# Second pair's mask rows on ScalarE's DMA queue, its preparation one step nearer, slot zeros from the second pair on

## The chip, the cores and the metric

The kernel runs on one core of a Trainium2 chip. The metric is device time in microseconds (us) of one launch, given as the median of several executions. A profile is one more execution, with its own time.

## The reference

Three layers follow each other: clustered attention, a mixture of experts with a carried choice of expert, and a gated causal convolution. Only the first, on which the change bears, is shown with more than a line.

```python
# q, k, v: 2 x 8 heads x 768 x 64; centroids: 8 heads x 16 x 64
q_assign = argmax(einsum('bhsd,hcd->bhsc', q_n, c_n)); k_assign = likewise for k
mask = q_assign[:, :, :, None] == k_assign[:, :, None, :]
scores = where(mask, 0.125 * q @ k^T, -1e9); attn = softmax(scores)
x = attn @ v                       # heads joined to 512 columns, 1536 tokens
e = argmax(x @ w_gate), or the expert of the token before where a local gate says so
y[token] = softmax(logits)[e] * (relu(x @ w1[e]) @ w2[e])
out = (sigmoid(causal_conv(y)) * (y @ w_val)) @ w_out
```

## The kernel before

**Attention, step by step.** The 16 heads are worked in 8 pairs of two heads. A pair has 12 items (2 halves of the queries, 3 tiles of 128 queries, 2 heads), so there are 96 items and 96 steps of one loop (L750). Step i issues the scores of item i+2 (S, L609 and L613: two matmuls over 128 rows and two over 80 rows, with a row maximum on VectorE, L620), the six transposes of item i on TensorE (T, L644), their two copies out of PSUM (L647 on VectorE or L649 on ScalarE; `act_only` says which), and the exponential of item i+2 on ScalarE (E, L629). From step 7 on, every odd step also issues the products with v of the half before (L656). Every engine executes its own instructions strictly in the order in which this loop writes them; nothing reorders them.

**The operands of the scores.** For each head of a pair there is a tile `st` with four planes of 768 columns: high and low parts of k and q over 128 rows, and in rows 64 to 79 of planes 2 and 3 the *mask rows*, the one-hot clusters of q and k. The last two score matmuls (L613, 80 rows) read them, so a masked score is built by TensorE itself. The first two (L609) do not need them.

**Preparation of the next pair (`prep_steps`).** Its parts, in six groups that the loop hands out one per step: (0) `k_hi` on ScalarE (L333) and `dots1` on TensorE (L351), which reads both halves of `xkq`, the loaded k and q; (1) `q_hi` on ScalarE (L336), `k_lo` on GpSimd (L339), `dots2` on TensorE (L361); (2) the argmax over clusters on VectorE, first part; (3) `q_lo` on VectorE (L342) and `stack1`, six DMAs of 384 KB that copy the parts into both `st` tiles (L406 to L408); (4) argmax, second part; (5) `rows` on TensorE (L390), `rows_out` on ScalarE (L400, writes `ohr`), and `stack2` for both heads, four DMAs of 48 KB that copy the mask rows from `ohr` into `st` (L412, L413). The index of the group is `i % 12 - (0 if g else 2)`: in the first pair, g = 0, the preparation of the second pair runs in steps 2 to 7; in later pairs it runs in steps 0 to 5 of the pair. The first item of the second pair is item 12, whose S is issued in step 10.

**Loads and zeros.** All of the DMAs named so far are issued by SyncE (SP), in program order. `xkq` and `vt` of the second pair are issued ahead of the loop (L82, L83, L88); `xkq` of the third in step 8. `fill_slots` (L148 to L158) writes zeros and a padding number to the two DRAM tables of token slots, 13 DMAs of 514 KB, one at each of the steps 0, 1, 10 and 11 of a pair until they are used up; ahead of the first, GpSimd sets the source tile `padrow`. Tokens are scattered into these tables from step 57 on. Step 7 of the first pair also converts the convolution's weights (`conv_weights`): seven small instructions on VectorE, one on ScalarE (L265), and two on VectorE that wait for it (L266, L267).

Of the kernel before, what the change touches and what calls it, by code (L numbers as in the profile page):

```python
# [8 lines left out]
F32 = mybir.dt.float32  # L9
# [23 lines left out]
def routed_attention_moe_kernel(  # L33
# [12 lines left out]
    nc = tc.nc  # L46
# [277 lines left out]
    def prep_steps(g):  # L324
# [3 lines left out]
        st = [st_p.tile([128, 4, S], F32R, tag=f"st{h}", name=f"st{h}") for h in range(2)]  # L328
# [80 lines left out]

        def stack2(h):  # L410
            r = o["ohr"].bitcast(F32)
            nc.sync.dma_start(st[h][64:80, 2, :].bitcast(F32), r[32 + 16 * h:48 + 16 * h, :])  # L412
            nc.sync.dma_start(st[h][64:80, 3, :].bitcast(F32), r[16 * h:16 * h + 16, :])  # L413

        def S0(h, parts=None):

# [186 lines left out]
    def do_S(i):  # L603
        g, qb, t, h = items[i]
        st = ST[g][h]
        q0 = 384 * qb + 128 * t
        ps = ps_s.tile([128, 2, 512], F32, tag="s", name="s")
        for n in range(2):
            nc.tensor.matmul(  # L609
                ps[:, n, :384], st[:, 1, q0:q0 + 128], st[:, 0, 384 * n:384 * n + 384], start=True, stop=False  # L610
            )
        for n in range(2):
            nc.tensor.matmul(  # L613
                ps[:, n, :384], st[0:80, 2, q0:q0 + 128], st[0:80, 3, 384 * n:384 * n + 384], start=False, stop=True
            )
        row_max(i, ps)
# [6 lines left out]
    def do_exp(i):  # L623
        g, qb, t, h = items[i]
        ps, mx = S_.pop(i)
        if (t, h) == (0, 0):
            Zt[i // 6] = small.tile([128, 3, 2], F32, tag="z", name="z", bufs=4)
        pt = p_p.tile([128, 2, 384], F32, tag="p", name="pexp", bufs=3)
        nc.scalar.activation(  # L629
            pt, ps[:, :, :384], AF.Exp, bias=mx[:, 0:1], accum_out=Zt[i // 6][:, t, h:h + 1]  # L630
        )
        P_[i] = pt.rearrange("p a b -> p (a b)")

    def do_T(i, act_only):
        g, qb, t, h = items[i]
        u = i // 6
        if t == 0:
            PT[u, h] = pt_p.tile([128, NQT, 384], F32, tag=f"pt{h}", name=f"pt{h}")
        p = P_.pop(i)
        for half in range(2):  # L640
            tp = ps_t.tile([128, 3, 128], F32, tag="t", name="tp")
            for k in range(3):
                kt = 3 * half + k
                nc.tensor.transpose(tp[:, k, :], p[:, 128 * kt:128 * kt + 128], ident)  # L644
            dst = PT[u, h][:, 3 * half:3 * half + 3, 128 * t:128 * t + 128]
            if half == 0 and not act_only:
                nc.vector.tensor_copy(dst, tp)  # L647
            else:
                nc.scalar.copy(dst, tp)  # L649

    def do_PV(u, kt):
        g, qb = items[6 * u][:2]
        if kt == 0:
            PVs[u] = ps_v.tile([128, 384], F32, tag="pv", name="pv")
        for h in range(2):
            nc.tensor.matmul(  # L656
                PVs[u][64 * h:64 * h + 64, :], Vt[g][:, kt, h, :], PT[u, h][:, kt, :],
                start=(kt == 0), stop=(kt == NQT - 1), skip_group_check=True,
            )
# [3 lines left out]
    def post1(u):  # L663
        ut = u_p.tile([128, 384], F32, tag="u", name="ut")
        nc.scalar.copy(ut, PVs.pop(u))  # L665
        U_[u] = ut
        for h in range(2):
            PT.pop((u, h))

    def post2(u):  # L670
        g, qb = items[6 * u][:2]
        b, p = pairs[g]
        ut = U_.pop(u)
        z = Zt.pop(u)
        rz = small.tile([128, 3, 2], F32, tag="rz", name="rz")
        nc.vector.tensor_scalar(rz, z, 1e-9, None, op0=ALU.add)
        nc.vector.reciprocal(rz, rz)
        po = ps_m.tile([128, 512], F32, tag="m", name="po")
        pv = po[:, :438].rearrange("p (t c) -> p t c", t=3)
        for t in range(3):  # L680
            nc.tensor.matmul(pv[:, t, :], ut[:, 128 * t:128 * t + 128], wgl_sb[:, p, :], start=True, stop=True)
        t0 = 6 * b + 3 * qb
        nc.vector.tensor_tensor(
            lall[:, t0:t0 + 3, 2 * p:2 * p + 2, :],
            pv[:, :, 128:146].rearrange("p t (h c) -> p t h c", h=2),
            rz.unsqueeze(3).to_broadcast([128, 3, 2, 9]), op=ALU.mult,
        )
        nc.vector.tensor_tensor(
            xnat[:, t0:t0 + 3, 128 * p:128 * p + 128].rearrange("p t (h d) -> p t h d", h=2),
            pv[:, :, 0:128].rearrange("p t (h d) -> p t h d", h=2),  # L690
            rz.unsqueeze(3).to_broadcast([128, 3, 2, 64]), op=ALU.mult,
        )
# [57 lines left out]
    for i in range(NI):  # L750
        g, qb, t, h = items[i]
        u, j = divmod(i, 6)
        if i % 12 == 0:
            prep = prep_steps(g + 1) if g + 1 < 8 else []
        if i + 2 < NI:
            do_S(i + 2)
        do_T(i, act_only=i % 12 in (2, 3, 4, 5, 6, 9) or u >= U - 1)
        if i + 2 < NI:
            do_exp(i + 2)
        if u == U - 1:  # L760
            if j < 2:
                for kt in range(3):
                    do_PV(u - 1, 3 * j + kt)
            if j == 1:
                post1(u - 1)
        elif u and j % 2:
            for kt in (j - 1, j):
                do_PV(u - 1, kt)
            if j == 5:
                post1(u - 1)  # L770
        ps = i % 12 - (0 if g else 2)
        if 0 <= ps < len(prep):
            for f in prep[ps]:
                f()
        if i in (54, 66):
            route = route_steps(i // 12 - 4)
        if j == (0 if u == U - 1 else 4 if i // 12 in (4, 5) else 3) and u > 1:
            post2(u - 2)
        if i == 6 * U - 4:
            post2(u - 1)  # L780
            route = route_steps(2)
        if 6 <= i % 12 <= 9 and i // 12 in (4, 5) or 2 <= j and u == U - 1:
            for _ in range((1, 3, 2, 3)[i % 12 - 6 if i // 12 in (4, 5) else j - 2]):
                route.pop(0)()
        if u == U - 1 and j >= 2:
            if j in (2, 4):
                last_PV(j // 2 - 1)
        if i % 12 == 8 and g + 2 < 8:
            load_kq(g + 2)
        if i % 12 == 7 and 0 < g < 7:  # L790
            load_v(g + 1)
        if i % 12 in (0, 1, 10, 11):
            next(fill, None)
        if i == 7:
            conv_weights()
        if i == 82:
            w_dma(0)
        if i in (84, 88):
            w_split(0, (i - 84) // 4, nc.gpsimd)
        if i == 90:  # L800
            w_dma(1)
# [495 lines left out]
```

## Time and profile before

| | |
|---|---|
| time, median of 3 executions | 572.93 us (572.6 to 576.06) |
| profiled execution: its own time | 573.4 us |
| profiled execution: span of the profile | 571.7 us (1.7 us of the time lie around it) |
| busy: TensorE, ScalarE, VectorE, GpSimd | 546.9, 338.9, 386.9, 115.1 us |
| mean granted clock of TensorE | 0.982 of full speed |
| first pair, steps 0 to 11 | from 18.3 us to about 48 us of the span |

Times inside the profile are us from the start of its span. In a timeline row stand the start, the duration, the engine (PE is TensorE's matmuls, PEld its weight loads, DVE VectorE, ACT ScalarE, POOL GpSimd; SPq and ACTq are the DMA issues of SyncE's and ScalarE's queues), the line, the operation with what it writes and reads, how many instructions are merged into the row, and in brackets the engine's idle time just before and what ended it. A DMA issue's duration is the time that its queue's sequencer was taken up, not the transfer's.

### The profile page before, as it was taken

Reading aid. Unit: us, or ns where it says so; the run is one execution under the profiler, and the core shown is the slowest. Engines: PE = TensorE matmul, PEld = TensorE weight load, DVE = VectorE, ACT = ScalarE, POOL = GpSimd, SP = SyncE. Lnnn points to the kernel's source line nnn. Section 1 sums busy time; section 2 is a strip of 40 time slices with the busy share of each in tenths; the row PEclk is TensorE's granted clock in tenths of the full one; section 3 lists DMA queues with packets and bytes.
Section 4 is the critical chain, followed back from the end, with each engine's and each line's share of the span. In section 5 each row is a group of like instructions: output and inputs, shape, how many; then the busy total and the mean of one; then the engine's idle time right before and its main releaser. Section 6 shows DMA issues by size and latency. Waiting matters only on the chain. (4 is left out here: it accounts for less than half of the span.)

```text
span 571.7 us, 9383 instructions
## 1 busy us (share of the span) xinstructions
PE 546.9 (96%) x3485; PEld 439.8 (77%) x3485; DVE 386.9 (68%) x661; ACT 338.9 (59%) x611; POOL 115.1 (20%) x105
## 2 busy tenths in 40 slices
PE   7888999999999999997999999999999998799996
PEld 4656767676777677765898989989899885599885
DVE  6575757676787876556378779687687581679950
ACT  3686777777768686862155656555555353465632
POOL 4101010101021210304350531504325225000000
PEclk8899999999999999997999999999999999899999
DMA  6977777673655646022648678777697955900022
GB/s 150 266 172 234 160 239 166 203 158 106 145 174 120 200 95 186 1 75 89 236 147 317 228 267 294 257 271 249 214 316 247 353 188 219 358 8 2 29 83 110
DMA packets 33103, 104.82 MB, mean 183 GB/s; under 512 B 5713, under 2 KB 6225, under 8 KB 27936
## 3 DMA queue, kind: packets, MB, share of 16 engines
q1 hardware_dynamic: 28816, 97.31, 55.0%
q0 software_dynamic: 3280, 6.32, 3.0%
q8 instruction: 28, 0.46, 0.3%
q10 hardware_dynamic: 960, 0.58, 0.3%
q14 instruction: 19, 0.16, 0.1%
HBM read 63.45 MB, written 24.95 MB: 155 GB/s over the span
## 5 line engine op out<-in xcount | busy, mean ns | idle before, releaser
L620 DVE TENSOR_REDUCE mx<-s 128x1 f32<-128x768 f32 x96 | 91.5, 954 | 60.8 <-PE s L613 54.4
L321 DVE TENSOR_TENSOR wlo<-wraw,whi 128x1024 fp32r<-128x1024 f32 x66 | 90.5, 1372 | 23.6 <-ACT whi L320 22.9
L649 ACT COPY pt<-tp 128x384 f32<-128x384 f32 x148 | 65.8, 484 | 54.8 <-PE tp L644 54.6
L629 ACT ACTIVATE pexp<-s,mx 128x768 f32<-128x768 f32 x96 | 87.2, 909 | 7.5 <-DVE mx L620 5.8
L320 ACT CAST whi<-wraw 128x1024 fp32r<-128x1024 f32 x68 | 70.3, 1046 | 31.6 <-DMA wraw<-in_wq_dram 31.3
L644 PE MATMUL tp<-ident,pexp 128*128 128x128 f32 x576 | 81.2, 277 | 0.6 <-DVE pt L647 0.3
L644 PEld LDWEIGHTS tp<-ident,pexp 128*128 128x128 f32 x576 | 67.9, 141 | 8.2 <-ACT pt L649 3.4
L656 PE MATMUL pv<-pt,vt 128*64 128x384 f32 x360 | 67.8, 498 | 0.2 <-ACT ut L665 0.2
L609 PE MATMUL s<-st 128*128 128x384 f32 x188 | 57.3, 386 | 1.8 <-ACT pexp L629 1.8
L987 PE MATMUL yp<-whi,hhi 128*128 128x512 f32 x136 | 53.8, 395 | 0.0
L991 PE MATMUL yp<-whi,hlo 128*128 128x512 f32 x136 | 53.7, 395 | 0.0
L990 PE MATMUL yp<-wlo,hhi 128*128 128x512 f32 x136 | 53.7, 395 | 0.0
L613 PE MATMUL s<-st 80*128 80x384 f32 x188 | 49.2, 343 | 2.8 <-DMA st<-ohr 2.6
L964 ACT ACTIVATE hhi<-hps 128x512 fp32r<-128x512 f32 (+1 forms) x36 | 20.7, 576 | 48.1 <-PE hps L960 43.5
L609 PEld LDWEIGHTS s<-st 128*128 128x128 f32 x188 | 28.6, 191 | 18.2 <-ACT pt L649 6.8
L960 PE MATMUL hps<-xhi,whi 128*128 128x256 f32 x256 | 41.5, 283 | 0.7 <-ACT xhi L934 0.7
L965 DVE SCALAR_TENSOR_TENSOR hlo<-hps,hhi 128x512 fp32r<-128x512 f32 (+1 forms) x36 | 23.6, 655 | 27.2 <-ACT hhi L964 24.3
L960 PE MATMUL hps<-xlo,whi 128*128 128x256 f32 x256 | 40.7, 280 | 0.1
L960 PE MATMUL hps<-xhi,wlo 128*128 128x256 f32 x256 | 40.4, 279 | 0.0
L656 PEld LDWEIGHTS pv<-pt,vt 128*64 128x64 f32 x360 | 21.9, 136 | 24.1 <-issue 23.7
L339 POOL TENSOR_TENSOR xx<-xkq,xx 128x768 fp32r<-128x768 f32 x8 | 14.6, 1823 | 120.4 <-ACT xx L333 120.4
L238 POOL TENSOR_TENSOR wspace<-wspace 128x512 f32<-128x512 f32 x8 | 14.3, 1783 | 117.9 <-ACT wspace L234 107.4
(225 smaller groups left out, 978.4 us busy)
## 6 DMA issues: line engine op xcount, KB each, us to landing
wraw<-in_wq_dram SPq DMA_DIRECT2D x34, 1024.0 KB, 4.8
st<-xx SPq DMA_DIRECT2D x48, 384.0 KB, 6.9
xkq<-in_kq_dram SPq DMA_DIRECT2D x15, 384.0 KB, 4.5
xslots<-padrow SPq DMA_DIRECT2D x8, 514.0 KB, 7.8
wspace<-in_wd_dram SPq DMA_DIRECT2D x8, 512.0 KB, 5.4
xs<-xslots SPq DMA_DIRECT2D x7, 514.0 KB
vt<-in_v_dram SPq DMA_DIRECT2D x8, 384.0 KB, 6.8
out_dram<-os SPq DMA_DIRECT2D x11, 256.0 KB, 2.0
```

The costliest lines, as they stand in the source:

```text
L320: nc.scalar.copy(hi[:, c], t[:, c])
L321: (lo_eng or nc.vector).tensor_tensor(lo[:, c], t[:, c], hi[:, c].bitcast(F32), op=ALU.subtract)
L609: nc.tensor.matmul(ps[:, n, :384], st[:, 1, q0:q0 + 128], st[:, 0, 384 * n:384 * n + 384], start=True, stop=False)
L620: nc.vector.tensor_reduce(mx, ps[:, :, :384], axis=AX.XY, op=ALU.max, negate=True)
L629: nc.scalar.activation(pt, ps[:, :, :384], AF.Exp, bias=mx[:, 0:1], accum_out=Zt[i // 6][:, t, h:h + 1])
L644: nc.tensor.transpose(tp[:, k, :], p[:, 128 * kt:128 * kt + 128], ident)
L649: nc.scalar.copy(dst, tp)
L656: nc.tensor.matmul(PVs[u][64 * h:64 * h + 64, :], Vt[g][:, kt, h, :], PT[u, h][:, kt, :], start=(kt == 0), stop=(kt == NQT - 1), skip_grou ...
L960: nc.tensor.matmul(hp[:, fi, :w], a[:, d, fs], c[:, d, :w], start=(n + d == 0), stop=(n + d == 5))
L987: nc.tensor.matmul(yp[t], hhi[:, fa, ts], whv[:, f, :], start=(q == 0 and f == 0), stop=False)
L990: nc.tensor.matmul(yp[t], hhi[:, fa, ts], wlv[:, f, :], start=False, stop=False)
L991: nc.tensor.matmul(yp[t], hlo[:, fa, ts], whv[:, f, :], start=False, stop=(q == 1 and f == 3))
```

## The change

Three edits. `stack2` of the second pair (g is the pair that is prepared, so g == 1) issues its four DMAs from ScalarE's queue; all other pairs' stay with SyncE. The preparation of the second pair starts at step 1 in place of step 2, so it takes steps 1 to 6. And `fill_slots` is not stepped in the first pair: its 13 DMAs stand at steps 12, 13, 22 to 25, 34 to 37 and 46 to 48, in place of 0, 1, 10 to 13, 22 to 25 and 34 to 36.

```diff
         def stack2(h):
             r = o["ohr"].bitcast(F32)
-            nc.sync.dma_start(st[h][64:80, 2, :].bitcast(F32), r[32 + 16 * h:48 + 16 * h, :])
-            nc.sync.dma_start(st[h][64:80, 3, :].bitcast(F32), r[16 * h:16 * h + 16, :])
+            eng = nc.scalar if g == 1 else nc.sync
+            eng.dma_start(st[h][64:80, 2, :].bitcast(F32), r[32 + 16 * h:48 + 16 * h, :])
+            eng.dma_start(st[h][64:80, 3, :].bitcast(F32), r[16 * h:16 * h + 16, :])
...
-        ps = i % 12 - (0 if g else 2)
+        ps = i % 12 - (0 if g else 1)
...
-        if i % 12 in (0, 1, 10, 11):
+        if g and i % 12 in (0, 1, 10, 11):
             next(fill, None)
```

The first place is TensorE at the start of the second pair's preparation. `s` is the score of an item, `tp` a half of an item's transposes, `dott` the result of `dots1`; before, T of item 1, S of item 4, T of item 2, `dots1`, S of item 5:

```order
L613 MATMUL s_332<-st1_195 128x384 x2
L644 MATMUL tp_340<-ident_140,pexp_303 128x128 x3
L644 MATMUL tp_345<-ident_140,pexp_303 128x128 x3
L609 MATMUL s_353<-st0_194 128x384 x2
L613 MATMUL s_353<-st0_194 128x384 x2
L644 MATMUL tp_360<-ident_140,pexp_326 128x128 x3
L644 MATMUL tp_365<-ident_140,pexp_326 128x128 x3
L351 MATMUL dott_373<-xkq_293,cd_116 32x384 x4
L609 MATMUL s_380<-st1_195 128x384 x2
```

and in the changed program:

```order
L614 MATMUL s_328<-st1_195 128x384 x2
L645 MATMUL tp_336<-ident_140,pexp_303 128x128 x3
L645 MATMUL tp_341<-ident_140,pexp_303 128x128 x3
L351 MATMUL dott_349<-xkq_293,cd_116 32x384 x4
L610 MATMUL s_356<-st0_194 128x384 x2
L614 MATMUL s_356<-st0_194 128x384 x2
L645 MATMUL tp_363<-ident_140,pexp_326 128x128 x3
```

`dots1` moved ahead of S of item 4 and T of item 2; lines after the edit are numbered one higher.

The second place is ScalarE behind `rows_out` (L400). `pt` are the copies of the transposes, `pexp` the exponential; before:

```order
L649 COPY pt_487<-tp 128x3x128
L629 ACTIVATE pexp,z<-s,mx 128x768
L400 ACTIVATE ohr<-pr,rowb 64x768
L265 ACTIVATE cw_521<-ct_518 128x20
L649 COPY pt_463<-tp 128x3x128
```

and in the changed program:

```order
L650 COPY pt_462<-tp 128x3x128 x2
L630 ACTIVATE pexp,z<-s,mx 128x768
L400 ACTIVATE ohr<-pr,rowb 64x768
L413 DMA st_306<-ohr 16x768
L414 DMA st_306<-ohr 16x768
L413 DMA st_307<-ohr 16x768
L414 DMA st_307<-ohr 16x768
L650 COPY pt_495<-tp 128x3x128
L630 ACTIVATE pexp,z<-s,mx 128x768
L265 ACTIVATE cw_516<-ct_513 128x20
L650 COPY pt_462<-tp 128x3x128
```

Four DMA issues now stand between `rows_out` and the copy and exponential of the next step, and L265 stands behind that exponential.

The third place is SyncE's queue from the loads of v to the third pair's load; before:

```order
L88 DMA vt<-in_v_dram 128x768 x2
L156 DMA xslots<-padrow 128x2x514 x2
L406 DMA st_306<-xx 64x1536
L407 DMA st_306<-xx 64x2x768
L408 DMA st_306<-xx 64x2x768
L406 DMA st_307<-xx 64x1536
L407 DMA st_307<-xx 64x2x768
L408 DMA st_307<-xx 64x2x768
L412 DMA st_306<-ohr 16x768
L413 DMA st_306<-ohr 16x768
L412 DMA st_307<-ohr 16x768
L413 DMA st_307<-ohr 16x768
```

and in the changed program:

```order
L88 DMA vt<-in_v_dram 128x768 x2
L406 DMA st_306<-xx 64x1536
L407 DMA st_306<-xx 64x2x768
L408 DMA st_306<-xx 64x2x768
L406 DMA st_307<-xx 64x1536
L407 DMA st_307<-xx 64x2x768
L408 DMA st_307<-xx 64x2x768
L82 DMA xkq<-in_kq_dram 128x768
L83 DMA xkq<-in_kq_dram 128x768
L156 DMA xslots<-padrow 128x2x514 x2
```

The two fills ahead of `stack1` and the four mask rows behind it have left this queue, and two fills in place of four stand behind the third pair's load.

## Rows read from the trace of the kernel before

**Rows 1.** Waits from 0 to 110 us: engine, line, waited for, total, times, longest

```profile
PE s L613 <- DMA st<-ohr: 2.6, 1, 2.6
```

**Rows 2.** Timeline, 34 to 48 us, at the border from first to second pair

```profile
39.02 1.90 SPq L412 DMA_DIRECT2D st<-ohr  x1
...
41.16 0.62 PE L609 MATMUL s<-st 128*128 128x384 f32 x2
...
43.26 0.59 SPq L413 DMA_DIRECT2D st<-ohr  x1
...
44.41 0.59 PE L613 MATMUL s<-st 80*128 80x384 f32 x2 [2.63 <-DMA st<-ohr]
```

**Rows 3.** Timeline, 0 to 110 us, steps 2 to 5 of the first pair

```profile
22.97 0.59 PE L609 MATMUL s<-st 128*128 128x384 f32 x2
...
24.59 1.16 PE L351 MATMUL dott<-xkq,cd 128*32 128x384 f32 x8
24.90 0.15 PEld L351 LDWEIGHTS dott<-xkq,cd 128*32 128x32 f32 x6 [0.17 <-DMA xkq<-in_kq_dram]
...
25.68 0.62 PE L609 MATMUL s<-st 128*128 128x384 f32 x2
...
26.14 0.86 ACT L333 CAST xx<-xkq 128x768 fp32r<-128x768 f32 x1
...
27.02 0.86 ACT L649 COPY pt<-tp 128x384 f32<-128x384 f32 x2
...
29.44 0.85 ACT L649 COPY pt<-tp 128x384 f32<-128x384 f32 x2
...
31.06 0.88 ACT L649 COPY pt<-tp 128x384 f32<-128x384 f32 x2
```

**Rows 4.** Timeline, 34 to 48 us, around the mask rows of the second pair

```profile
36.33 0.99 ACT L400 ACTIVATE ohr<-pr,rowb 64x768 fp32r<-64x768 bf16 x1
...
37.05 1.86 SPq L408 DMA_DIRECT2D st<-xx  x1
37.22 0.21 ACT L265 ACTIVATE cw<-ct 128x20 f32<-128x20 int32 x1
37.46 0.18 DVE L266 TENSOR_TENSOR cw<-cw,ct 128x20 f32<-128x20 f32 x1 [0.75 <-ACT cw L265]
```

**Rows 5.** Timeline, 0 to 110 us, the first DMA issues of both queues

```profile
0.79 0.39 SPq L92 DMA_DIRECT2D cent_sb<-in_cent_dram  x1
0.79 0.42 ACTq L83 DMA_DIRECT2D xkq<-in_kq_dram  x1
```

**Rows 6.** Stretches, 1 us: PE, PEld, DVE, ACT, POOL busy; clock; DMA share; GB/s

```profile
17.00:18.00 1.00, 0.00 (x0) 0.00 (x0) 1.00 (x2) 0.71 (x1) 0.00 (x0) 1.00 1.04 212
...
19.00:20.00 1.00, 1.00 (x9) 0.96 (x7) 0.66 (x1) 0.16 (x2) 0.00 (x0) 0.75 1.01 218
20.00:21.00 1.00, 0.91 (x4) 0.40 (x2) 0.76 (x2) 0.69 (x2) 0.00 (x0) 0.50 0.89 258
21.00:22.00 1.00, 0.91 (x3) 0.81 (x4) 0.00 (x0) 0.69 (x2) 0.00 (x0) 0.50 0.81 289
22.00:23.00 1.00, 1.00 (x8) 1.00 (x6) 0.86 (x1) 0.00 (x0) 0.00 (x0) 0.54 0.90 249
...
42.00:43.00 1.00, 0.00 (x0) 0.00 (x0) 0.00 (x0) 0.00 (x0) 0.00 (x0) 1.00 0.88 209
```

**Rows 7.** Timeline of SyncE's queue, 0 to 130 and 110 to 260 us

```profile
84.47 0.51 SPq L406 DMA_DIRECT2D st<-xx  x1
...
102.07 1.90 SPq L156 DMA_DIRECT2D xover<-padrow  x3
113.97 0.51 SPq L406 DMA_DIRECT2D st<-xx  x1
...
143.54 0.51 SPq L406 DMA_DIRECT2D st<-xx  x1
```

## The prediction

> **What bounds the kernel now.** I read the waits of the first 110 us, then the timeline around the longest wait of TensorE, then the steps ahead of it, then short stretches for the clock, and last SyncE's queue over several pairs. The change touches only the first pair and the order of DMAs up to the fourth, so those are the places that count. In the waits one line stands out: TensorE waits 2.6 us, once, for a DMA of mask rows [rows 1]. The timeline shows it at the border of the pairs [rows 2]. The first two matmuls of item 12, the first item of the second pair, start at 41.16 and end at 41.78; the two that read mask rows start at 44.41, after 2.63 us idle. The mask rows were issued from 39.02 on, because SyncE's queue was still pushing the six large copies ahead of them: the last of those took its sequencer from 37.05 to 38.91 [rows 4], although `rows_out` had finished on ScalarE at 37.32. All engines run this loop in order, so the 2.63 us are on the path; nothing later gives them back. They are the most that this change can win at this place.
>
> In the steps ahead, ScalarE sets the pace: from 29.44 to 31.06 it does one step, two copies and one exponential, in 1.62 us [rows 3], without a gap.
>
> **Part one: the preparation one step nearer.** Moved are `k_hi`, `dots1`, `q_hi`, `k_lo`, `dots2`, the argmax, `q_lo`, the six copies, `rows` and `rows_out`; none is added. `dots1` cannot follow. Before, its matmuls start at 24.59 and stop for the second half of `xkq`, and the rest goes on at 24.90, when that load lands [rows 3]. So the old place was already the earliest that the load allows. In the changed order `dots1` stands directly behind T of item 1, at about 22.97, where S of item 4 started before, and holds TensorE, with everything queued behind it (S of item 4, T of item 2), until 24.90. The fills that go were issued behind `xkq` on the same queue, so I take the landing as unchanged. `dots1` then ends as before, and at 25.68 S of item 4 starts in place of S of item 5. ScalarE fills a part of the hole with `k_hi` (0.86, which stood at 26.14), then idles, and at 27.02 it copies T of item 2 where it had copied T of item 3. From there both streams look alike, each item one step late: the preparation keeps its old times, and the items lose one step, 1.62 us. Bounds: 0 if the load lands 1.9 us earlier than its row shows, 1.62 if it lands as shown. I take 1.62. `stack1` and `rows_out` come out at their old times within some tenths, since `q_hi`, `q_lo` and the argmax hang on the same landing.
>
> **Part two: four mask-row issues on ScalarE.** They wait for `rows_out`, which ScalarE has just written, and queued behind them on ScalarE are a copy of T of item 7, the exponential of item 9 and L265. For the copy waits T of item 8, for the exponential T of item 9, and for L265 VectorE, whose L266 and L267 stand ahead of the row maximum of item 10; before, that wait was 0.75 us [rows 4]. So ScalarE's loss goes into the chain in full; in this stretch nothing else covers it. The cost: the same transfer takes SyncE's queue 0.59 us when that queue is empty, as at the last of the four [rows 2], so four are 4 x 0.59 = 2.36 us. ScalarE's queue has nothing else in flight then. Bounds: 0, if copies and exponential have slack enough to hide it (nothing excludes that the first issue overlaps the end of `rows_out`); on the other side 4 x 1.90 = 7.6 us, if each takes what the first took on SyncE's loaded queue. I take 2.36, the row of the empty queue being the nearest.
>
> The landing is no longer what is late: issued from about 37.3 to 39.7, the rows would need more than 5 us to land to matter, because S of item 12 now comes at 41.16 + 1.62 + 2.36 = 45.1. The six large copies, whose issue ends by 38.9 as before, are then there; the waits name a single stop of this kind [rows 1], so what follows item 12 did not wait for them even before.
>
> A rule of the skill bears on this. In the rows, both queues issue side by side: at 0.79 SyncE for 0.39 us and ScalarE for 0.42 us, at the same start [rows 5]. The Trainium skill, page Perfetto Trace Analysis, section DMA Instruction — HWDGE (DVE, Sync), says that an issue first locks a shared descriptor generator for exclusive use, and that this lock wait is part of the profiled duration; by that, ScalarE's issues would stand in line behind SyncE's long ones, which is the rival below, while by the row they cost 2.36 us. The trace does not show two long issues at once, so it agrees only weakly with either.
>
> **Part three: the fills.** Two 514 KB fills leave the time of steps 0 and 1, two that of steps 10 and 11, and all come later by up to twelve steps. They cost nothing where they go: a pair with three fills takes from 84.47 to 113.97, 29.50 us, and the next, without any, from 113.97 to 143.54, 29.57 us [rows 7]. They gave nothing where they stood: no engine waits for a transfer behind them. The last is written at step 48, ahead of the first scatter at step 57. The setting of `padrow` moves on GpSimd, which is nearly idle. I take 0 for the whole part; bounds -0.3 and +0.3 from the spread of the two pairs.
>
> **The sum.** The stall goes, -2.63; the items lose a step, +1.62; ScalarE's issues, +2.36; fills 0: together +1.35, which I round to +1.3. The profiled execution took 573.4 us (571.7 of span and 1.7 around it), so it would be 574.7. It lies 0.47 above the median of the runs, 572.93; against that the forecast is 574.2. One per cent, 5.7 us, is about what a measurement of this kernel can tell from no change, so this is no change.
>
> **Rivals.**
>
> *The issues are hidden.* If ScalarE's issues overlap with work that waits anyway, the sum is -2.63 + 1.62 = -1.0, so 571.9. For it: behind the stall ScalarE has idle time. Against: in the steps ahead it has none [rows 3], and the issues stand right behind them.
>
> *ScalarE's issues stand in line with SyncE's.* Place: ScalarE behind `rows_out`, while SyncE still pushes the six large copies. Price: the same four issues took SyncE from 39.02 to 43.85 [rows 2], 4.8 us, so 2.5 more than I took: +3.8, 576.7; at 1.90 each, 7.6 us, it is +6.6, 579.5. It decides from the point where one issue takes more than about 1.7 us (then the whole is slower by 1%). For it: SyncE's third and later large issues do take 1.9 us. Against: the side-by-side issue at 0.79.
>
> *The clock falls once more.* After TensorE's idle time around 17 the granted clock went from 1.00 to 0.50, that is from 2.4 to 1.2 GHz, from 19 to 23, and took 0.25 + 0.50 + 0.50 + 0.46 = 1.71 us of full speed [rows 6]. The new stop from about 23.2 to 24.9 is of that length. Price +1.7 at most, since ScalarE sets the pace there: +3.0 in all, 576.0. Against: after the longer stop at 42 the clock stayed at 1.00 [rows 6].
>
> *The change does not do what it says.* The rows could still land last, if a packet on ScalarE's queue waited for all of SyncE's backlog; then S of item 12 goes on near 44.4 to 45.8, which is the forecast's time again.
>
> **How the numbers follow.** Forecast as worked out, 0.45; hidden issues 0.17; standing in line 0.16; a second fall of the clock 0.18; something else 0.04. The range from 571.3 to 577.3 holds the first two, the clock and the cheaper half of the line, with some tenths for the measurement; left out are the dear half of the line and half of the unknown. Slower by over 1% (above 578.7): the dear part of the line and a little of the unknown, 0.05. Faster by over 1% (below 567.2): 0.02, for which this stretch has no room. Within 1%: 0.93.
>
> **What would show it.** In the changed profile: `dots1` starts near 23 and its second part after 24.9, with 1.5 to 2 us of TensorE idle for `xkq`; S of item 4 starts near 25.7; no wait of L614 for `ohr`; four issues on ScalarE's queue of about 0.6 us each from 37 on; the first S of the second pair near 45. It would be wrong if `dots1` ran through at 23 (the load came earlier), if the four issues took 1 us or more each, if the clock were 0.50 after 25, or if the second pair's first scores came before 43.

## The result, and the profile after

| | before, beside it | after |
|---|---|---|
| median of 8 executions each | 575.25 us (572.6 to 577.9) | 578.32 us (577.14 to 580.83) |
| after / before, 95% interval | | 1.0065 [1.0043, 1.0088] |
| profiled execution: its own time | 573.4 us | 577.14 us |
| profiled execution: span | 571.7 us | 575.4 us |

The changed kernel is slower by 0.65%, or 2.5 to 5.1 us of 575.25; that is within 1%, but the time lies above the forecast and above its range. Of the 4.1 us between the forecast of 574.2 and 578.32, 2.3 are the starting point: the forecast began at 572.93, the median of three executions, and the same kernel took 575.25, the median of eight, beside the changed one. The other 1.8 are the change itself, which cost 3.1 where 1.3 was forecast. The kernel before took 574.19 to 578.87 us as a median in the sets of runs below, so everything from here on is compared by ratio within a set, or by places inside one profile.

The place that tells most is the first large copy of a pair on SyncE's queue (L406 in both files; lines behind the first edit stand one higher in the changed file). It waits for the pair's `q_hi`, so it shows how late the preparation, and with it the loop, runs. In the timeline of SyncE's queue, the one for the third pair stands in the kernel before at

```profile
54.98 0.51 SPq L406 DMA_DIRECT2D st<-xx  x1
```

and in the changed kernel those for the third, the fourth and the sixth pair stand at

```profile
59.47 0.48 SPq L406 DMA_DIRECT2D st<-xx  x1
...
88.95 0.51 SPq L406 DMA_DIRECT2D st<-xx  x1
...
148.01 0.51 SPq L406 DMA_DIRECT2D st<-xx  x1
```

At the third pair, a copy that before started at 54.98 starts at 59.47: 4.49 us late. At the fourth pair the lag against [rows 7] is 4.48, at the sixth 4.47. So all of the loss arises before 59, in the stretch that the prediction looked at, and the fills, which now stand in the second to fifth pair, add nothing there. The end comes only 3.7 us later. The lag falls from 4.5 to 3.9 between 260 and 300, where the clock is low for 6.8 us before and for 3.4 in the changed kernel, and to 3.7 at 490, where the clock is low before (487 to 490.5) and not in the changed kernel. Such late stretches differ from profile to profile; 3.7 and 4.49 both lie in the interval.

The waits of the changed kernel from 35 to 50 us no longer name the mask rows [rows 1]. The longest ones now hang on ScalarE. The timeline in that stretch:

```profile
34.80 0.98 ACT L400 ACTIVATE ohr<-pr,rowb 64x768 fp32r<-64x768 bf16 x1
...
35.12 1.51 PE L657 MATMUL pv<-pt,vt 128*64 128x384 f32 x8
...
35.68 1.88 SPq L408 DMA_DIRECT2D st<-xx  x1
35.80 0.58 ACTq L413 DMA_DIRECT2D st<-ohr  x1
...
36.42 2.00 ACTq L414 DMA_DIRECT2D st<-ohr  x1
...
38.46 1.98 ACTq L413 DMA_DIRECT2D st<-ohr  x1
40.48 0.84 ACTq L414 DMA_DIRECT2D st<-ohr  x1
...
41.36 0.48 ACT L650 COPY pt<-tp 128x384 f32<-128x384 f32 x1 [5.59 <-issue]
...
41.89 0.55 PE L645 MATMUL tp<-ident,pexp 128*128 128x128 f32 x3 [4.03 <-ACT pt L650]
...
42.78 1.01 PE L610 MATMUL s<-st 128*128 128x384 f32 x2 [0.35 <-ACT pexp L630]
42.87 0.18 DVE L266 TENSOR_TENSOR cw<-cw,ct 128x20 f32<-128x20 f32 x1 [5.71 <-ACT cw L265]
...
45.64 2.83 PE L657 MATMUL pv<-pt,vt 128*64 128x384 f32 x8
...
48.40 1.01 PE L610 MATMUL s<-st 128*128 128x384 f32 x2
```

`rows_out` ends at 35.78. The four issues on ScalarE's own queue (ACTq) then take 0.58, 2.00, 1.98 and 0.84 us, with what lies between them 35.80 to 41.32: 5.5 us in which ScalarE does nothing else. Behind them stands the copy of a half of the transposes, which starts at 41.36 after "5.59 <-issue". TensorE needs that copy for its next three transposes and starts them at 41.89, after 4.03 us idle. VectorE's L266, behind L265, waited 5.71 us where it waited 0.75 before [rows 4]. From 42.5 on, matmuls take longer: the first two of an S 1.01 us in place of 0.62 [rows 2], the eight products with v 2.83 in place of 1.51 at 35.12. The first S of the second pair starts at 48.40, against 41.16 before [rows 2].

The stretches 36 to 42 and 42 to 50 (columns as in [rows 6]) of the changed kernel:

```profile
36.00:42.00 6.00, 1.97 (x12) 1.14 (x9) 1.02 (x8) 0.64 (x2) 0.00 (x0) 1.00 1.01 224
42.00:50.00 8.00, 7.65 (x29) 4.96 (x30) 2.74 (x6) 4.00 (x10) 0.00 (x0) 0.57 0.76 242
```

and of the kernel before:

```profile
36.00:42.00 6.00, 5.50 (x36) 3.50 (x33) 3.19 (x10) 4.44 (x11) 0.00 (x0) 1.00 0.99 215
42.00:50.00 8.00, 5.44 (x34) 3.97 (x35) 2.96 (x5) 3.24 (x7) 0.00 (x0) 1.00 0.81 238
```

TensorE is busy for 1.97 us of the first six where it was busy for 5.50, and then its granted clock is 0.57 on average where it was 1.00: taken by single microseconds it is 0.50, which is 1.2 GHz, from 42.5 to 49.3.

### The profile page after: what moved, and what is told of

Read it like the earlier page. It is cut to its first block, busy times and chain, and to the rows that moved or that the text cites. A ratio compares the mean times of both kernels' runs of the same rounds, so it can differ in the third digit from the quotient of the medians.

```text
span 575.4 us, 9376 instructions
## 1 busy us (share of the span) xinstructions
PE 548.0 (95%) x3485; PEld 440.6 (77%) x3485; DVE 385.9 (67%) x661; ACT 338.2 (59%) x611; POOL 115.3 (20%) x105
## 3 DMA queue, kind: packets, MB, share of 16 engines
HBM read 63.45 MB, written 24.95 MB: 154 GB/s over the span
## 5 line engine op out<-in xcount | busy, mean ns | idle before, releaser
L321 DVE TENSOR_TENSOR wlo<-wraw,whi 128x1024 fp32r<-128x1024 f32 x66 | 88.9, 1349 | 24.8 <-ACT whi L320 24.4
L657 PE MATMUL pv<-pt,vt 128*64 128x384 f32 x360 | 69.1, 507 | 0.1
L614 PE MATMUL s<-st 80*128 80x384 f32 x188 | 49.6, 345 | 0.0
L966 DVE SCALAR_TENSOR_TENSOR hlo<-hps,hhi 128x512 fp32r<-128x512 f32 (+1 forms) x36 | 23.6, 656 | 27.3 <-ACT hhi L965 27.3
```

What stands on the lines that cost most here:

```text
L321: (lo_eng or nc.vector).tensor_tensor(lo[:, c], t[:, c], hi[:, c].bitcast(F32), op=ALU.subtract)
L657: nc.tensor.matmul(PVs[u][64 * h:64 * h + 64, :], Vt[g][:, kt, h, :], PT[u, h][:, kt, :], start=(kt == 0), stop=(kt == NQT - 1), skip_grou ...
```

## Experiments

Each kernel is named by its ratio to the kernel before in the same set of runs, with a 95% interval, and by the start of the third pair's first large copy, 54.98 before and 59.47 after (the *mark* below). The shift of the mark lies inside the interval of the ratio for the ten kernels below that were timed more than once, and for the changed kernel. A mark is read from one profile, so it also holds what that execution did earlier: the start of `rows_out` (L400) tells how much. It is 34.80 in the changed kernel and 34.82 to 34.95 in all but three of the kernels below with the nearer preparation. "Landed" stands for the time at which the last of the sixteen parts of a transfer reports its end, which the traces keep. The theory after reading the trace (A): the issues on ScalarE hold that engine, the stop makes TensorE's clock fall, and the rest of the change gains a little. The letters in the quoted expectations stand for explanations: A is this one, G says that the load lands near 23.6 whatever is behind it, M that an issue waits until the DMA engines have drained queued copies; what another letter holds is said where it stands. Each diff is against the changed kernel, where nothing else is said. No kernel leaves out a part of the computation; three of them add useless work, named with them.

**Rows back on SyncE's queue (edits 2 and 3 alone).**

```diff
-            eng = nc.scalar if g == 1 else nc.sync
+            eng = nc.sync
```

> The change without its first edit: the second pair's mask rows stay on SyncE's queue; preparation one step nearer and fills from the second pair on are kept. Theory A (ScalarE is held by its own four issues, and TensorE's low clock follows from the stop): ScalarE is not held, the first copy after rows_out follows within 0.6 us, the clock stays at 1.00 around 42, the large copies end as in the changed kernel (near 37.6), the mask rows are issued from there on and land some 5 us later, so the first scores of the second pair go on near 42.8 in place of 44.41 before: about 1.5 us faster than before, ratio 0.997. Theory B (the nearer preparation or the moved fills cost the time): still 3 to 4.5 us slower than before, ratio 1.006.

0.9958 [0.992, 0.9996]; mark 53.66, 1.32 earlier than before. Its timeline at the border:

```profile
39.70 1.62 SPq L414 DMA_DIRECT2D st<-ohr  x1
...
43.09 0.59 PE L614 MATMUL s<-st 80*128 80x384 f32 x2 [1.38 <-DMA st<-ohr]
...
53.66 0.51 SPq L406 DMA_DIRECT2D st<-xx  x1
```

Without the issues on ScalarE the loss is gone and the rest of the change is a gain. The stop of S of item 12 has not gone, but is 1.38 us in place of 2.63. That gives 1.25 of the 1.32.

**Rows on ScalarE's queue alone (edit 1 alone).**

```diff
-        ps = i % 12 - (0 if g else 1)
+        ps = i % 12 - (0 if g else 2)
...
-        if g and i % 12 in (0, 1, 10, 11):
+        if i % 12 in (0, 1, 10, 11):
```

> The first edit alone: the second pair's mask rows from ScalarE's queue, preparation and fills as before. Theory A: the four issues take ScalarE 5 to 6 us from 37.3 on, TensorE stops about 4 us and its clock falls behind the stop, the second pair starts 4 to 6 us later than before: ratio 1.007 to 1.010. Theory B: no more than 2.4 us of issues and no wait for the mask rows, so the time of before or up to 2.6 us less: ratio 0.996 to 1.001.

1.0075 [1.0044, 1.0106]; mark 60.27, 5.29 later than before. `rows_out`, the first two issues, and TensorE's stop:

```profile
37.47 0.99 ACT L400 ACTIVATE ohr<-pr,rowb 64x768 fp32r<-64x768 bf16 x1
...
38.49 0.59 ACTq L413 DMA_DIRECT2D st<-ohr  x1
...
39.12 1.90 ACTq L414 DMA_DIRECT2D st<-ohr  x1
...
44.58 0.90 PE L645 MATMUL tp<-ident,pexp 128*128 128x128 f32 x3 [4.87 <-ACT pt L650]
```

The other two issues took 1.97 and 0.82 us. `rows_out` is already 1.14 us later than in [rows 4]; in this execution the low clock of the start lasted to 25.8, before to 22.9. So about 4.15 of the 5.29 come behind it. The harm is in this edit. It does not need the preparation to be moved, nor the fills.

**The same four DMAs from GpSimd's queue.**

```diff
-            eng = nc.scalar if g == 1 else nc.sync
+            eng = nc.gpsimd if g == 1 else nc.sync
```

> The changed kernel with the second pair's mask rows issued from GpSimd's queue in place of ScalarE's. Theory A: GpSimd has nothing waiting behind it, ScalarE is free, so the hold of 5.5 us goes and the clock stays; the rows bypass SyncE's queue, so the first scores of the second pair go on between 41 and 43: 1.5 to 3 us faster than before, ratio 0.995 to 0.998. Theory B: as the changed kernel, 3 to 4.5 us slower than before.

0.9951 [0.9915, 0.9987]; mark 53.50.

```profile
36.23 0.73 POOL L413 DMA_DIRECT2D st<-ohr  x1 [5.87 <-ACT ohr L400]
...
36.97 0.51 POOL L414 DMA_DIRECT2D st<-ohr  x1
...
43.04 0.59 PE L614 MATMUL s<-st 80*128 80x384 f32 x2 [1.21 <-DMA st<-ohr]
```

GpSimd has nothing queued behind the issues, so the four, 2.2 us, cost nothing. But the rows land no earlier. Item 12 reads those of the first head: on GpSimd's queue their two issues end at 37.48, they landed at 42.68 and 42.95, and S goes on at 43.04; on SyncE's the issues end at 41.32, they landed at 42.60 and 42.95, and S goes on at 43.09. Being issued 3.8 us earlier on a queue of their own did not bring the rows sooner, and the last large copy landed later, at 44.53 against 42.33. (SyncE, free of the rows, also issues the third pair's load earlier there, from 37.82 in place of 42.68, so the rows and the copies share with that as well.) The Trainium skill, page DMA: Bandwidth & Descriptors, section "Issuing engines are not separate DMA queues", says that DMAs of all three issuers run on the same 16 engines and interleave there; these landings agree with it.

**TensorE kept busy during the stop.** Sixteen useless matmuls are added in step 8, in front of its transposes; the issues stay on ScalarE.

```diff
+        if i == 8:
+            keep_warm(ps_m.tile([128, 512], F32, tag="m", name="spin9"), 16)
         do_T(i, act_only=i % 12 in (2, 3, 4, 5, 6, 9) or u >= U - 1)
```

> The changed kernel with 16 more matmuls of no use on TensorE in step 8, between the scores and the transposes, where TensorE otherwise stands still for 4.03 us; about 3.5 us of work in that hole. Theory A: ScalarE is held as long as in the changed kernel, but the clock stays at 1.00 behind the hole, and the second pair starts about 2 us earlier than in the changed kernel: ratio to before 1.003 to 1.004 in place of 1.0065. If the low clock costs nothing because ScalarE sets the pace there, the time of the changed kernel.

1.0012 [0.9982, 1.0043]; mark 57.44, 2.03 earlier than the changed kernel's.

```profile
37.49 3.63 PE L104 MATMUL spin<-onesb 128*128 128x512 bf16 x16
...
40.57 0.95 ACTq L414 DMA_DIRECT2D st<-ohr  x1
...
40.96 0.49 PE L645 MATMUL tp<-ident,pexp 128*128 128x128 f32 x3
```

The four issues on ScalarE are as long as ever (0.58, 1.99, 1.95 and 0.95), but the useless matmuls fill 3.63 us of the stop, the granted clock stays at 1.00 up to 50, and 2.03 us come back. They delay nothing themselves: the transposes behind them end at 41.45, and ScalarE's last issue at 41.52. This is the price of the low clock at this place, in this pair of executions. With the kernel above that has the rows on SyncE's queue, the whole lag falls into three steps of the mark: 54.98 to 53.66, -1.32 for the nearer preparation; to 57.44, +3.78 for ScalarE held; to 59.47, +2.03 for the clock. Together +4.49. `rows_out` starts within 0.13 us in these three kernels, so the last two steps do not come from earlier in their profiles.

**The preparation one step nearer alone (edit 2).**

```diff
-            eng = nc.scalar if g == 1 else nc.sync
+            eng = nc.sync
...
-        if g and i % 12 in (0, 1, 10, 11):
+        if i % 12 in (0, 1, 10, 11):
```

> The second edit alone: preparation of the second pair one step nearer; mask rows on SyncE's queue, fills as before. Theory F (the fills, issued behind the second pair's load, slow it): dots1 starts near 23 and stops until the load lands near 24.9, the items lose 1.2 to 1.6 us, and the mask rows come out as before, so the time stays within 0.5 us of before: ratio 0.999 to 1.001. Theory G (the load lands near 23.6 whatever is behind it, and before the change TensorE merely came later): dots1 runs through near 23.7, and the kernel is 1.3 us faster than before, as with fills moved: ratio 0.996 to 0.998.

0.9977 [0.9941, 1.0014], so no difference that the ratio can show; mark 53.68, 1.30 earlier. `dots1`:

```profile
23.48 1.02 PE L351 MATMUL dott<-xkq,cd 128*32 128x384 f32 x8
```

All eight matmuls run through from 23.48, with the fills still right behind the load. Four of the eight read its second half, so it was there by about 24.0 (half of the 1.02 us on), 0.9 us ahead of 24.90; it landed at 23.61. And this edit alone makes the gain of 1.3 in the mark, of which up to 0.3 can be the late load of the profile of before, where `dots1` took 1.16 us; in the kernel with the rows on SyncE's queue it ran through in 0.85.

**The fills alone (edit 3).** The diff is against the kernel before.

```diff
-        if i % 12 in (0, 1, 10, 11):
+        if g and i % 12 in (0, 1, 10, 11):
```

> The third edit alone: no fills in the first pair; preparation in steps 2 to 7 and mask rows on SyncE's queue as before. Theory F: the second pair's load lands by 23.6, ahead of dots1 in its old place near 24.5, so nothing but the stop of 0.2 us there goes; the large copies run from the same times, the mask rows still land near 44: ratio 0.999 to 1.000. Theory G: the same. If fills in the first pair cost more than that (four fewer at the border of the pairs), 0.996 to 0.998.

1.0 [0.9967, 1.0033]; mark 55.08, and S of item 12 still stops for 2.50 us. The fills are worth nothing, either way. `dots1`, at its old place in this kernel, has this row:

```profile
25.00 0.16 PEld L351 LDWEIGHTS dott<-xkq,cd 128*32 128x32 f32 x8 [0.17 <-issue]
```

No wait for the load shows here, because TensorE came to `dots1` only at 25.00. But the load had landed just before, at 24.95, though no fill stood behind it. With the fills behind it, in the kernel above, it had landed at 23.61. So the fills do not decide when it lands, and neither does it always land near 23.6, as G has it.

**The third pair's load held back.** Why does an issue of 48 KB take 2 us? While ScalarE issues, SyncE issues the load of the third pair. In this kernel the load waits for a useless one-column copy on VectorE in step 8, so that SyncE has nothing to issue then.

```diff
-        if i % 12 == 8 and g + 2 < 8:
-            load_kq(g + 2)
+        if i == 8:
+            dmy = small.tile([128, 1], F32, tag="dmy", name="dmy")
+            nc.vector.tensor_copy(dmy, X[1][:, 0, 0:1])
...
+        if i % 12 == 8 and g + 2 < 8:
+            load_kq(g + 2)
```

> The changed kernel with the third pair's load held back on SyncE's queue until a one-column copy of the old load's tile on VectorE in step 8 is done, so that SyncE issues nothing from 37.6 until ScalarE is through. Theory L (ScalarE's issues take turns with SyncE's issues): the first issue takes 0.6, the second up to 2.0 beside SyncE's last large copy, the third and fourth 0.6 each: 3.8 us in all in place of 5.5, and the hold ends near 39.7. Theory M (each issue behind the first waits until the DMA engines have drained what is queued, whoever queued it): the third still takes about 2 us, since the large copies drain until about 41.9: 5 us or more in all, and the time of the changed kernel. Under L TensorE's stop shrinks to about 2.3 us, the second pair starts 1.7 us or, if the clock stays up, 3 us earlier than in the changed kernel: ratio 1.001 to 1.004; under M 1.005 to 1.008.

1.0044 [1.0014, 1.0074]; mark 58.37.

```profile
35.81 1.86 SPq L408 DMA_DIRECT2D st<-xx  x1
35.91 0.58 ACTq L413 DMA_DIRECT2D st<-ohr  x1
...
36.53 1.96 ACTq L414 DMA_DIRECT2D st<-ohr  x1
...
38.53 1.93 ACTq L413 DMA_DIRECT2D st<-ohr  x1
40.51 0.89 ACTq L414 DMA_DIRECT2D st<-ohr  x1
...
44.80 0.33 SPq L82 DMA_DIRECT2D xkq<-in_kq_dram  x1
```

SyncE issues nothing from 37.67 to 44.80, and ScalarE's four take 0.58, 1.96, 1.93 and 0.89, as in the changed kernel. So they did not take turns with issues of SyncE. What remains is that they wait for room, which the large copies already queued give back only as they are moved. That fits the pace of the copies, which landed at 37.15, 39.71, 41.92 and 43.84, 1.9 to 2.6 us apart. But it is reached by elimination and not shown directly.

The mark is 1.10 us earlier than the changed kernel's, though TensorE stops for as long (4.00 us). The clock fell at 40.1 here, inside the stop, so 1.9 of its 6.8 us at 0.50 passed while TensorE stood still. Against the kernel with useless matmuls (57.44) that leaves 0.93 for the clock, where the changed kernel had 2.03: the price depends on when the fall comes. No kernel tested this alone.

**Another order on SyncE's queue.** Edits 2 and 3, the rows on SyncE, and the two copies that need only `k_hi` and `q_hi` issued earlier, so that the rows of the first head stand ahead of the second head's last copies.

```diff
-            eng = nc.scalar if g == 1 else nc.sync
+            eng = nc.sync
...
+        def stack0(h):
+            r = slice(64 * h, 64 * h + 64)
+            nc.sync.dma_start(st[h][0:64, 0:2, :].bitcast(F32), xx[r, 0:2, :].bitcast(F32))
...
-            nc.sync.dma_start(s[0:64, 0:2, :].bitcast(F32), xx[r, 0:2, :].bitcast(F32))
+            if g != 1:
+                stack0(h)
...
+                [q_hi, k_lo, dots2, lambda: stack0(0), lambda: stack0(1)],
+                [argmax1, argmax2],
+                [q_lo, lambda: stack1(0)],
+                [argmax3, argmax4],
+                [rows, rows_out, lambda: stack2(0), lambda: stack1(1), lambda: stack2(1)],
```

> The second and third edits with the mask rows on SyncE's queue, and SyncE's copies for the second pair in another order: both copies of planes 0 and 1 right behind q_hi, then the other two of head 0, its mask rows, then the other two of head 1 and its mask rows. With the mask rows on SyncE's queue in the old order the first scores of the second pair still stopped 1.38 us for them, and from GpSimd's queue 1.21 us, because the rows share the DMA engines with the large copies. If only what is queued ahead of them decides, the rows of head 0 now land near 38 to 39, the stop goes, the last copy of head 1 ends near 41.5 and the second pair starts another 1.3 us earlier: 2.6 us before the kernel before, ratio 0.992 to 0.995. If the rows land late for another reason, the stop stays: 0.995 to 0.998.

0.9947 [0.9921, 0.9973]; mark 53.04, the earliest of all. The stop that is left:

```profile
44.18 0.60 PE L628 MATMUL s<-st 80*128 80x384 f32 x2 [1.11 <-DMA st<-ohr]
```

S of item 12 no longer stops; S of item 13, which reads the second head's rows, does, for 1.11 us.

**All four rows ahead of the second head's last copies.** The diff is against the kernel above.

```diff
-                [rows, rows_out, lambda: stack2(0), lambda: stack1(1), lambda: stack2(1)],
+                [rows, rows_out, lambda: stack2(0), lambda: stack2(1), lambda: stack1(1)],
```

> As the kernel with the reordered copies, but all four mask rows stand together, ahead of the last two large copies of head 1. There the stop moved from item 12 to item 13, 1.11 us for the mask rows of head 1. If what is queued ahead of the rows decides, neither item 12 nor item 13 now waits for them, the last copy of head 1 lands near 43 when item 13 wants it, and the third pair's first copy is issued about 1 us earlier than there, at about 52 (before: 54.98): ratio 0.991 to 0.994. If the large copies, now later by four small ones, become the stop, about as there: 0.994 to 0.996.

0.9973 [0.9948, 0.9997]; mark 53.76, so this is no step further (`rows_out` came 0.34 us later in this execution than in the one above, and the mark 0.72). The last row's issue, and the stop:

```profile
38.08 0.58 SPq L419 DMA_DIRECT2D st<-ohr  x1
...
44.88 0.62 PE L628 MATMUL s<-st 80*128 80x384 f32 x2 [1.45 <-DMA st<-xx]
```

The rows are out by 38.66, and what item 13 waits for is now a large copy (`st<-xx`), for 1.45 us. The first of the two expected cases, 0.991 to 0.994, was missed; the second came true: with the rows in front, the large copies become the last to land.

**Only the first head's rows on ScalarE.**

```diff
-            eng = nc.scalar if g == 1 else nc.sync
+            eng = nc.scalar if g == 1 and h == 0 else nc.sync
```

> The changed kernel with only head 0's two mask rows on ScalarE's queue and head 1's on SyncE's: half of the suspected hold. Theory M (each issue behind the first waits until the engines have drained what is queued): 0.6 and 2.0 us, ScalarE held 2.6 us in place of 5.5, TensorE stops 1 to 1.5 us, the clock stays at 1.00, and the third pair's first copy is issued near 55 (changed kernel 59.47, before 54.98, rows on SyncE's queue 53.66): ratio 0.998 to 1.000. If the hold comes from ScalarE having any transfer at all queued there, or the clock falls again, near 57 to 59: 1.003 to 1.006.

1.0029 [1.0008, 1.005]; mark 56.44, where about 55 was expected.

```profile
24.29 0.15 PEld L351 LDWEIGHTS dott<-xkq,cd 128*32 128x32 f32 x6 [1.64 <-DMA xkq<-in_kq_dram]
...
36.52 0.58 ACTq L413 DMA_DIRECT2D st<-ohr  x1
...
37.13 1.99 ACTq L414 DMA_DIRECT2D st<-ohr  x1
...
39.70 0.55 PE L645 MATMUL tp<-ident,pexp 128*128 128x128 f32 x3 [1.12 <-ACT pt L650]
...
40.59 0.62 PE L610 MATMUL s<-st 128*128 128x384 f32 x2 [0.35 <-ACT pexp L630]
```

The hold is halved, as expected: two issues, 2.6 us. But the granted clock was 0.50 from 42.0 for 3.4 us all the same, after TensorE had stood still for 1.12 us behind ScalarE and then for 0.35. That was one of the expected cases, but not the one that M gives. Of the difference between 55 and 56.4 about half at most can be put down to it: the second pair's load landed late in this execution, at 24.25, `dots1` stopped 1.64 us for it, and `rows_out` starts at 35.52, 0.72 us later than in the changed kernel. No kernel tried the rest by itself.

**Four issues on ScalarE beside one copy.** The kernel with the rows on SyncE, and in step 3 four useless issues of the rows' size on ScalarE's queue, where SyncE has queued only one large copy. The diff is against the kernel with the rows on SyncE's queue. It was profiled once and not timed further.

```diff
+        if i == 3:
+            for r in range(4):
+                nc.scalar.dma_start(quiet[16 * r:16 * r + 16, :], X[1][16 * r:16 * r + 16, 0, :])
```

> The kernel with the mask rows on SyncE's queue and the other two edits, plus four issues of no use on ScalarE's queue in step 3 (16 rows of the second pair's loaded k to a scratch tile, the size of a mask row each), where at most one large copy is queued. Theory M: 0.4 to 0.7 us each, 1.6 to 2.8 us in all, where the same four took 5.5 us behind six large copies. If a small transfer on ScalarE's queue takes 2 us by itself from the second on, 5 us and more.

576.12 us, one execution.

```profile
29.36 0.58 ACTq L798 DMA_DIRECT2D quiet<-xkq  x1
29.38 0.48 SPq L406 DMA_DIRECT2D st<-xx  x1
...
29.98 1.29 ACTq L798 DMA_DIRECT2D quiet<-xkq  x1
...
31.30 1.86 ACTq L798 DMA_DIRECT2D quiet<-xkq  x2
...
33.73 1.54 PE L645 MATMUL tp<-ident,pexp 128*128 128x128 f32 x6 [1.71 <-ACT pt L650]
```

The four take 0.58, 1.29 and, two in one row, 1.86 us: 3.7 us in all, between what an empty queue and what a loaded one would give. That leaves open what exactly an issue waits for. It shows only that even beside a single large copy the price is not 4 x 0.59. TensorE stops for 1.71 us behind it, and here too the granted clock is 0.50 from 33.0 on, for 6.8 us.

## Why the prediction was wrong

**The stop at the border** was read rightly as the largest thing in reach, and the changed kernel has no wait of L614 for `ohr`, as forecast. But it goes only because everything else is late by then: the rows landed at 40.99 to 45.29, 4.8 to 7.0 us after their issue began, and the forecast had it that they would have to take more than 5 to matter. With nothing held, it shrinks from 2.63 to 1.38 us on SyncE's queue and 1.21 on GpSimd's.

**Part one was off by more than its size.** The step "24.90, when that load lands" was read rightly for its execution: the load landed at 24.86 there, and TensorE, which had come to `dots1` at 24.59, waited for its second half inside it. The row ahead of that wait, before:

```profile
24.59 0.14 PEld L351 LDWEIGHTS dott<-xkq,cd 128*32 128x32 f32 x2 [0.17 <-issue]
```

What failed is the step behind it, "So the old place was already the earliest that the load allows". It took one execution's landing for every execution's. In the thirteen profiles of this document the same half of the load landed between 23.38 and 24.95, with the fills behind it and without; ten are at 23.68 or earlier. What makes it late in three of them is open. In the changed kernel `dots1` looks like this, with the copies of the transposes of items 2 and 4 behind it:

```profile
22.81 1.62 PE L351 MATMUL dott<-xkq,cd 128*32 128x384 f32 x8
...
23.58 0.15 PEld L351 LDWEIGHTS dott<-xkq,cd 128*32 128x32 f32 x6 [0.64 <-DMA xkq<-in_kq_dram]
...
25.70 0.86 ACT L650 COPY pt<-tp 128x384 f32<-128x384 f32 x2 [0.67 <-PE tp L645]
...
29.73 0.87 ACT L650 COPY pt<-tp 128x384 f32<-128x384 f32 x2
```

The second half of the load is there at 23.58, 1.3 us before the forecast's landing. TensorE stops for 0.64, not for 1.9. T of item 2 is copied at 25.70, where the forecast had 27.02; T of item 4 at 29.73, against 29.44 before [rows 3]. So the items lose 0.29, not 1.62, near the lower of the two bounds; and the preparation comes earlier by the rest, `rows_out` at 34.80 in place of 36.33 [rows 4], which the forecast had "at their old times". It does not always come out so: with only the first head's rows on ScalarE the load landed at 24.25, TensorE stopped for 1.64 us, and T of item 4 was copied at 30.45, so the items lost 1.0.

**Part two is the step that decided.** It priced the issues at "4 x 0.59 = 2.36 us", from the row of a queue taken for empty, with the reason that ScalarE's queue has nothing else in flight. The four took 5.5 us. SyncE's queue was not empty at its 0.59 either: the last large copy landed only at 43.73, though the other five were through. ScalarE's queue was empty, and copies of 384 KB were still being moved (in the changed kernel they landed at 37.02, 39.55, 41.77 and 43.69); by elimination it is these that an issue had to wait for. The nearer row was SyncE's own four behind the same copies, 4.8 us, which stands in the prediction as the rival's price. The engine that was held is the one that sets the pace, so most of it came into the chain, as the prediction said: +3.78 of the mark. Of the 1.7 that did not, 1.38 is the stop of S of item 12, which is still there without the hold and goes with it.

**The clock** was looked for at 23 to 25, after `dots1`. There it stayed at 1.00, with a stop of 0.64. It fell at 42.5, after the stop that the misjudged issues made, and cost 2.03 us, for which the sum had nothing. The prediction's argument against, a clock of 1.00 after the stop at 42 before [rows 6], held for that stop of 2.63 us and not for one of 4.03.

**Part three** was right: fills 0. Its bounds of 0.3 are wider than the spread of the two pairs that they cite, which is 0.07.

**The rivals.** "ScalarE's issues stand in line with SyncE's" had the place and, within 0.7 us, the price; its mechanism has fallen, for the issues are as long when SyncE issues nothing. Its point that SyncE's third and later large issues take 1.9 us is misread: before, the third took 0.59, the fourth 1.28, and only the last two 1.95 and 1.86. ScalarE's first issue ran from 35.80 to 36.38, inside SyncE's of 35.68 to 37.56, in no more than 0.58 us. The exclusive lock that the Trainium skill describes (page Perfetto Trace Analysis, section DMA Instruction — HWDGE (DVE, Sync)) would have made that first issue wait, if SyncE held it for most of its own. These two rows do not bear that out; how much of SyncE's 1.88 us was spent under such a lock they do not show. "The clock falls once more" had the right mechanism in the wrong place. What happened is both together, the one causing the other, and no case had that. "The issues are hidden" and "does not do what it says" fell.

**The signs named in advance** gave it away one by one: issues of 1 us or more (two of 2 us, 1.35 on average), a clock of 0.50 after 25, and a `dots1` whose load came early. The second pair's first scores came at 48.40, not near 45.

**The sum** had -2.63 + 1.62 + 2.36 = +1.35. In its place the mark shows -1.32 for preparation and stop together, where the sum had -1.01; +3.78 where it had 2.36; and +2.03 where it had nothing. So in part one the stop that did not go by itself (1.38) and the step that was not lost (1.33) cancel nearly, and the miss of the change's own cost is the issues, by 1.4, and the clock, by 2.0. One per cent was also too coarse for what can be told here: the interval of the ratio is 0.23% to either side.

Faster than both kernels, by about half a per cent against the one before, are the rows on SyncE's queue, on GpSimd's, or in the other order with the first head's rows ahead: 0.9958, 0.9951 and 0.9947, whose intervals overlap.

## What to carry to other kernels

Price a DMA issue by the same queue's rows while as much is in flight as there will be, not by an issue on an empty queue; and put it on an engine that has nothing waiting behind it, since here a second queue moved the issuing cost but did not bring the data sooner. A landing read in one profile is that execution's: ask how it varies over several before a step of a forecast rests on it. When a change makes TensorE stop for longer than it did, add to the stop the low clock that may follow it, which in the changed kernel cost half as much again (2.03 on 3.78).

## What the runs showed of the hardware that was not expected

- An issue of 48 KB took ScalarE up to 2.00 us on a queue that held nothing but such rows, while copies of 384 KB from another queue were under way; with SyncE issuing nothing it took 1.96. What limits it is open.
- Mask rows whose issues ended at 37.48 on GpSimd's queue and at 41.32 on SyncE's landed by 42.95 in both cases and released the same matmul at 43.04 and 43.09.
- TensorE's clock stayed at 2.4 GHz after one stop of 2.63 us before, and went to 1.2 GHz after one of 4.03; but it also fell behind stops of only 1.12 us (half of the rows on ScalarE) and 1.71 us (useless issues). The longest single stop does not tell alone whether it falls. In the kernel with the load held back it fell 2.1 us into a stop of 4.00 and cost about half as much (0.93 against 2.03).
- The same half of the second pair's load, issued within 0.3 us of the same time, landed between 23.38 and 24.95 in thirteen profiles; whether fills were queued behind it did not decide it.
